# The state read of an attention-and-experts kernel in 64x32 tiles over two banks, beside the small S.W group, with one ring of eight PSUM banks

## The chip, the cores and the metric

The kernel runs on one core of a Trainium2 chip. The metric is device time in microseconds (us) of one execution; the numbers are medians over several executions. A core has TensorE (PE in the profile; its weight loads are listed as PEld), VectorE (DVE), ScalarE (ACT), GpSimd (POOL) and SyncE (SP, which issues most DMAs). Matmul results land in PSUM, eight banks of 128 partitions with 512 float32 columns each, and VectorE or ScalarE copies ("evicts") them to SBUF.

## The reference

For each of 8 batches and 8 heads, `x` has 512 tokens of 64 features and `state` has 32 rows of 64. Both read each other with softmax attention; the two reads are laid one after the other as 544 rows per batch, heads side by side in 512 columns, and go through a two-expert layer with a maximum:

```python
scores = scale * np.matmul(x, state.transpose(0, 1, 3, 2))
a = softmax(scores)                        # over the 32 state rows
xread = np.matmul(a, state)
scores2 = scale * np.matmul(state, x.transpose(0, 1, 3, 2))
a2 = softmax(scores2)                      # over the 512 tokens
sread = np.matmul(a2, x)
attn = np.concatenate([xread, sread], axis=2)
...
h1 = attn_rows @ w1
h2 = attn_rows @ w2
out = np.maximum(h1, h2) @ w_out
```

(`softmax` stands for the lines that subtract the maximum, take the exponential and divide by the sum.) Inputs and output are float32; `w1` and `w2` are 512x1024, `w_out` is 1024x512.

## The kernel before

max(h1, h2) is computed as h2 + relu(h1 - h2): `wd` holds w1 - w2, `wo` holds w_out, and `wwo` holds w2 @ w_out. Since the rows of xread are a @ state, the kernel multiplies each batch's state by the weights first. In its names, for a batch `b`:

- `sc_mm`, `sc_ev`: the scores and their exponentials `e` (ScalarE, L233). `norm` (L237 to L241) divides by the sums; the result `a` is transposed by a DMA into `aT`.
- `sw_mm` (L309), the small S.W group: state times `wd` and `wwo`, in three blocks of 512 columns. Each block is 8 matmuls of 64 rows by 32 columns of weights, into two banks; 24 matmuls in all. `sw_ev` copies the six banks into `sw`, three by VectorE and three by ScalarE (L97, L95).
- `l1` (L339): 8 tiles of two matmuls, `sw` against `aT`, with the relu on ScalarE (L328) and VectorE (L330) in turn.
- `l2(b, c)` (L349 and L354): for each of 4 blocks of 128 tokens, two matmuls against the `wwo` part of `sw` and eight against `wo`; `l2_out` copies the bank to `h` (c even on VectorE, odd on ScalarE), and `store` writes four blocks out.
- `sr_mm` (L275), the state read: 32 matmuls per batch, weights `e` (128 rows, 32 columns, one of four column groups of the array), moving `xe` (65 columns: 64 features and a one, which gives the sum of the exponentials). All accumulate in one bank: 4 heads on the partitions, two head groups of 65 columns, or 130 columns per batch. `sr_ev` (L283 to L289) takes the reciprocal of the sums and scales; `sr_tr` (L293) transposes `sr`, and `sr_cp` puts it into `sread_t`, which is multiplied by the weights at the end (`m1`, `m2`).

The first stage, batch 0 and the weights, follows a written order (`ORDER`). After it comes a loop over b = 1 to 6, the passes, which issues in program order on each engine. Pass b does l1 of batch b, scores of batch n = b + 1, l2(0) and l2(1) of b, S.W of n, the state read, the evictions of both, l2(2), l2(3) and the transposes of sr. In pass 1 l1, the scores, l2(0) and l2(1) lie in the written order already. Passes 1 and 2 read two states each: `rd` is (n, b - 1). In the loop, banks come from two rings: "r" with banks 0 to 5 for l1, scores, S.W and the transposes, and "a" with banks 6 and 7 for l2 and the state read. A matmul that opens a bank waits until the bank's last contents have been read. After the loop batch 7 runs l1, `m1` and three blocks of l2 into held banks; a branch on a flag (sums out of range) guards a slower path, which these inputs do not take.

The order in the loop around the change:

```python
        pg = [sw_mm(n, 512 * z, 512 * z + 512) for z in range(3)]
        rd = (n, b - 1) if b < 3 else (n,)
        p = bank("a")
        for j, v in enumerate(rd):
            sr_mm(v, p, j)
        for z in range(3):
            sw_ev(pg[z], n, 512 * z, 512 * z + 512, "VA" if z % 2 == 0 else "AV")
        for j, v in enumerate(rd):
            sr_ev(p[:, 130 * j:130 * j + 130], v, "VA"[j])
```

Of the kernel before, what the change touches and what calls it, by code (L numbers as in the profile page):

```python
# [8 lines left out]
F32 = mybir.dt.float32  # L9
# [3 lines left out]
ALU = mybir.AluOpType  # L13
# [31 lines left out]
def kernel(  # L45
# [9 lines left out]
    nc = tc.nc  # L55
# [3 lines left out]
    DM = H * D  # L59
    FF = moe_w1.shape[1]  # L60
    NC = S // 128
# [22 lines left out]
    def bank(ring="r", dtype=F32):  # L84
        if isinstance(ring, int):
            i = ring
        else:
            r = rings[ring]
            i = r[turn[ring] % len(r)]
            turn[ring] += 1  # L90
        return banks[i] if dtype == F32 else banks[i].bitcast(BF16)
# [175 lines left out]
        copy(eng, at_tile(b)[:, g].rearrange("p c t -> p (c t)"), p[:, 0:512])  # L267


    def sr_mm(b, p, j=0):  # L270
        d = d_(b)
        for c in range(NC):
            for g in range(2):
                for k in range(4):
                    nc.tensor.matmul(p[32 * k:32 * k + 32, 130 * j + 65 * g:130 * j + 65 * g + 65], d["e"][:, g, c, k],  # L275
                                     d["xe"][:, c, k, 7 + 65 * g:72 + 65 * g],
                                     start=(j == 0 and c == 0 and g == 0), stop=(c == NC - 1 and g == 1),
                                     skip_group_check=True)

    def sr_ev(p, b, eng="V"):  # L280
        sr = at.tile([128, 2, D], BF16, tag="sr", bufs=3, name="sr")
        d_(b)["sr"] = sr
        nc.vector.reciprocal(rr_all[:, b], p[:, 0:130:129])  # L283
        for g in range(2):
            o, i, r = sr[:, g, :], p[:, 1 + 64 * g:65 + 64 * g], rr_all[:, b, g:g + 1]
            if eng == "A":
                nc.scalar.activation(out=o, in_=i, func=ACTF.Copy, scale=r)  # L287
            else:
                nc.vector.tensor_scalar(o, i, scalar1=r, scalar2=None, op0=ALU.mult)  # L289
# [67 lines left out]
    def l2_out(b, c, p, eng, lo=0, hi=DM):  # L357
        if b not in OB:
            OB[b] = h8(NC, DM)
        copy(eng, OB[b][:, c, lo:hi], p[:, lo:hi])  # L360

    def l2(b, c, eng=None, ring="a"):
        p = bank(ring)
        l2_open(b, c, p, True, False)
        l2_f(b, c, p, range(NF), False, True)
        l2_out(b, c, p, eng or ("A" if c % 2 else "V"))

    def store(b, c0=0, c1=NC, lo=0, hi=DM, eng=None):
        dst = out[b * L:b * L + S].rearrange("(p c) n -> p c n", c=NC)
# [76 lines left out]
    ps = {}  # L446
# [74 lines left out]
        step(tok)  # L521


    rings["r"], rings["a"] = [0, 1, 2, 3, 4, 5], [6, 7]
    turn["r"] = turn["a"] = 0
    for b in range(1, B - 1):
        n = b + 1
        if b > 1:
            if b + 2 < B:
                for g in range(2):  # L530
                    cast_b(b + 2, g, "P")
                xt_dma(b + 2)
            for f in range(NF):
                l1(b, f)
            pp = [sc_mm(n, hh) for hh in range(2)]
            for hh in range(2):
                sc_ev(pp[hh], n, hh)
            for hh in range(2):
                norm(n, hh, "P")
            at_dma(n)  # L540
        else:
            for g in range(2):
                cast_b(3, g, "P")
            xt_dma(3)
        if b > 2 and b + 2 < B:
            for k in range(4):
                cast_e(b + 2, k, "P")
        if b + 3 < B:
            for g in range(2):
                load_x(b + 3, g)  # L550
        if b > 1:
            l2(b, 0)
            l2(b, 1)
        pg = [sw_mm(n, 512 * z, 512 * z + 512) for z in range(3)]
        rd = (n, b - 1) if b < 3 else (n,)
        p = bank("a")
        for j, v in enumerate(rd):
            sr_mm(v, p, j)
        for z in range(3):
            sw_ev(pg[z], n, 512 * z, 512 * z + 512, "VA" if z % 2 == 0 else "AV")  # L560
        for j, v in enumerate(rd):
            sr_ev(p[:, 130 * j:130 * j + 130], v, "VA"[j])
        if b < 3:
            for k in range(4):
                cast_e(b + 2, k, "P")
        l2(b, 2)
        if n == B - 1:

            cl = at.tile([128, B * 34], F32, tag="cl", bufs=1, name="cl")
            ne = at.tile([128, B * 34], F32, tag="ne", bufs=1, name="ne")  # L570
            bad = at.tile([128, 1], BF16, tag="bad", bufs=1, name="bad")
            flag = at.tile([128, 1], I32, tag="flag", bufs=1, name="flag")
            sv = sums[:, 0:B * 34]
            nc.vector.tensor_scalar(cl, sv, scalar1=1e-20, scalar2=1e20, op0=ALU.max, op1=ALU.min)
            nc.vector.tensor_tensor(ne, cl, sv, op=ALU.not_equal)
            nc.vector.tensor_reduce(bad, ne, axis=AXX, op=ALU.max)
        l2(b, 3)
        for v in rd:
            sr_cp(sr_tr(v, "r"), v, "A")
        if n == B - 1:  # L580
            p = bank("r")
            nc.tensor.matmul(p[0:2, 0:1], ones, bad, start=True, stop=True)
            nc.vector.tensor_copy(flag[0:1, :], p[0:1, 0:1])
        store(b)
# [16 lines left out]
    with tc.If(nc.values_load(flag[0:1, 0:1], skip_runtime_bounds_check_because="compared with zero alone") >= 1):  # L601
        mx = at.tile([128, 2 * NC, 2], F32, tag="mx", bufs=1, name="mx")
        cm = at.tile([64, 2], F32, tag="cm", bufs=1, name="cm")
        e2 = at.tile([64, 512], BF16, tag="e2", bufs=1, name="e2")
        gx, gob, gd = h8(H, NC * D), h8(NC, DM), h8(NC, DM)
        dl = gd[:, 0, :]
        for v in range(B):
            st[v], AT[v], SW[v], R[v], xf_t[v] = st[b], AT[b], SW[b], R[b], gx
            if v < b:
                OB[v] = gob  # L610
            d = d_(v)
            for g in range(2):
                fetch_x(v, 4 * g, 4 * g + 4)
            for k in range(4):
                cast_e(v, k, "AV"[k % 2])
            for k in range(4):
                xt_ev(xt_mm(v, k), v, k, "AV"[k % 2])
            for hh in range(2):
                pv = sc_mm(v, hh).rearrange("p (c g i n) -> p g c i n", c=NC, g=2, i=2)
                for g in range(2):  # L620
                    m = mx[:, 4 * g:4 * g + 4]
                    dv = dl[:, 256 * g:256 * g + 256].rearrange("p (c i n) -> p c i n", c=NC, i=2)
                    nc.vector.tensor_reduce(m, pv[:, g], axis=AXX, op=ALU.max)
                    nc.vector.tensor_tensor(dv, pv[:, g], m.unsqueeze(3).to_broadcast([128, NC, 2, Ns]),
                                            op=ALU.subtract)
                nc.scalar.activation(out=e_view(v, hh), in_=dl.rearrange("p (m i n) -> p m i n", i=2, n=Ns),
                                     func=ACTF.Exp, scale=scale)
                norm(v, hh, "V")
            for g in range(2):
                at_ev(at_mm(v, g, "r"), v, g, "AV"[g])  # L630
            for k in range(4):
                p = bank("r")
                for c in range(NC):
                    nc.tensor.matmul(p[0:64, c * 128:(c + 1) * 128], sbd[:, v, k, :], d["xt"][:, c, k, :],
                                     start=(c == 0), stop=(c == NC - 1))
                nc.vector.tensor_reduce(cm[:, 0:1], p[0:64], axis=AXX, op=ALU.max)
                nc.vector.tensor_scalar(cm[:, 1:2], cm[:, 0:1], scalar1=-scale, scalar2=None, op0=ALU.mult)
                nc.scalar.activation(out=e2, in_=p[0:64], func=ACTF.Exp, bias=cm[:, 1:2], scale=scale)
                pt = bank("r", BF16)
                for c in range(NC):  # L640
                    nc.tensor.transpose(pt[:, c * 64:(c + 1) * 64], e2[:, c * 128:(c + 1) * 128], ident[0:64, 0:64])
                copy("V", d["e"][:, :, :, k, :], pt[:, 0:256].rearrange("p (c g n) -> p g c n", c=NC, g=2))
            p = bank("r")
            sr_mm(v, p)
            sr_ev(p, v)
            sr_cp(sr_tr(v, "r"), v, "A")
            for z in range(3):
                sw_ev(sw_mm(v, 512 * z, 512 * z + 512), v, 512 * z, 512 * z + 512)
            for f in range(NF):
                l1(v, f)  # L650
            if v < b:
                for c in range(NC):
                    l2(v, c, ring="r")
                store(v)
        for f in range(NF):
            m1(f)
        l2_held()
# [42 lines left out]
```

## Time and profile before

| | |
|---|---|
| Time, median of 3 runs | 151.7 us (150.84 to 152.78) |
| Time of the profiled execution | 152.39 us |
| Its span, first to last instruction | 150.6 us |
| Granted TensorE clock, mean | 0.993 |
| Busy: TensorE, its weight loads | 139.7 us, 70.4 us |
| Busy: VectorE, ScalarE, GpSimd | 84.8 us, 65.9 us, 50.8 us |

The profile is of one execution. Its timeline has a line for each run of like instructions: start in us from the span's start, length in us, engine, line of the kernel, operation, what it writes and reads, shape, count, and in brackets how long the engine had been idle and what ended that. The length reaches from the first start to the last end, and since matmuls are pipelined the next line's start can lie before it. Lines of groups have busy time in us and mean ns of one instruction, then the idle time before them. Below, S marks the start of the last matmul of l2(1) in a pass.

### The profile page before, as it was taken

To read this page: it belongs to the slowest core of one execution; us is meant where nothing else is said; L and a number is where in the kernel's file an instruction comes from. 1 tells how busy PE (TensorE), PEld (TensorE's weight loads), DVE (VectorE), ACT (ScalarE), POOL (GpSimd) and SP (SyncE) were. 2 spreads that over 40 slices of the span, in tenths; PEclk is the share of its full clock that TensorE was granted. 3 is DMA by queue.
4 is the path that set the end of the run, shared out by engine and by line. 5 is a ranking of instruction groups with operands and counts; after the bars stand their busy time and mean duration, and the time that the engine had idled before them with its cause. 6 is when DMAs were issued, how large, how long until landed. Compare 5 with 4: busy or idle time off the path is not lost. (4 is left out here: it accounts for less than half of the span.)

```text
span 150.6 us, 3166 instructions
## 1 busy us (share of the span) xinstructions
PE 139.7 (93%) x1262; PEld 70.4 (47%) x1281; DVE 84.8 (56%) x167; ACT 65.9 (44%) x129; POOL 50.8 (34%) x71
## 2 busy tenths in 40 slices
PE   6769899999999999999999999999999999998970
PEld 2446445544444445444544544454445444843450
DVE  3579787964717828563854676284838575502120
ACT  5233663664682546246540825371455417401100
POOL 3123223499002932862490556228201300000000
PEclk9999999999999999999999999999999999999997
DMA  4999999946916399899979977995823305000541
GB/s 106 297 371 362 362 351 360 340 105 109 264 52 279 72 140 354 275 138 362 281 133 212 343 144 71 282 318 100 74 120 159 60 16 246 35 11 7 209 172 41
DMA packets 36741, 29.11 MB, mean 193 GB/s; under 512 B 21616, under 2 KB 34160, under 8 KB 35824
## 3 DMA queue, kind: packets, MB, share of 16 engines
q1 hardware_dynamic: 36304, 28.64, 68.7%
q8 instruction: 12, 0.20, 0.5%
q10 hardware_dynamic: 416, 0.20, 0.5%
q14 instruction: 9, 0.07, 0.2%
HBM read 15.20 MB, written 8.91 MB: 160 GB/s over the span
## 5 line engine op out<-in xcount | busy, mean ns | idle before, releaser
L354 PE MATMUL bank<-wo,r 128*128 128x512 bf16 (+1 forms) x261 | 61.3, 373 | 0.6 <-issue 0.2
L354 PEld LDWEIGHTS <-r 128*128 128x128 bf16 x264 | 25.5, 98 | 28.9 <-issue 0.7
L95 ACT COPY h<-bank 128x512 f32<-128x512 f32 (+1 forms) x17 | 9.5, 574 | 48.3 <-PE bank L354 37.8
L339 PE MATMUL bank<-aT,sw 128*128 128x512 bf16 x128 | 30.1, 379 | 0.1
L330 DVE TENSOR_SCALAR r<-bank 128x512 bf16<-128x512 f32 x28 | 19.4, 692 | 17.5 <-PE bank L339 16.9
L328 ACT ACTIVATE r<-bank 128x512 bf16<-128x512 f32 x36 | 21.3, 612 | 7.3 <-PE bank L339 7.0
L241 POOL TENSOR_TENSOR a<-e,er 128x512 bf16<-128x512 bf16 x13 | 13.4, 1048 | 27.4 <-ACT e L233 15.6
L97 DVE CAST sw<-bank 128x512 bf16<-128x512 f32 (+1 forms) x25 | 15.1, 653 | 11.5 <-PE bank L309 11.5
L99 POOL CAST xb<-h 128x1024 bf16<-128x1024 f32 x12 | 12.4, 1039 | 18.5 <-issue 12.0
L339 PEld LDWEIGHTS <-sw 128*128 128x128 bf16 x128 | 12.0, 98 | 12.9
L99 POOL CAST xe<-h 128x512 bf16<-128x512 f32 x27 | 15.8, 622 | 6.5 <-DMA h<-in_x_dram 5.7
L97 DVE COPY h<-bank 128x512 f32<-128x512 f32 (+1 forms) x16 | 10.5, 659 | 12.4 <-PEq L601 6.5
L349 PE MATMUL bank<-sw,aT 128*128 128x512 bf16 (+1 forms) x53 | 16.1, 372 | 0.5 <-ACT sr L287 0.2
L95 ACT CAST sw<-bank 128x512 bf16<-128x512 f32 (+1 forms) x27 | 13.2, 559 | 6.2 <-PE bank L309 6.2
L233 ACT ACTIVATE e<-bank 128x512 bf16<-128x512 f32 x16 | 8.9, 595 | 5.5 <-PE bank L225 4.9
L237 DVE TENSOR_REDUCE sums<-e 128x16 f32<-128x512 bf16 x16 | 10.6, 663 | 1.1 <-ACT e L233 1.0
L426 PE MATMUL bank<-wo,w2t 128*128 128x512 bf16 x30 | 7.8, 380 | 0.8 <-DVE w2t L97 0.6
L433 PE MATMUL bank<-wz 128*128 128x256 bf16 (+1 forms) x38 | 7.4, 337 | 1.2 <-DVE ones L438 1.2
L349 PEld LDWEIGHTS <-aT 128*128 128x128 bf16 x66 | 5.5, 98 | 4.8 <-issue 0.7
L225 PEld LDWEIGHTS <-xt 128*128 128x128 bf16 x128 | 5.0, 98 | 2.1 <-ACT xt L95 0.3
L309 PE MATMUL bank<-wd,sbd 64*32 64x512 bf16 (+1 forms) x144 | 5.6, 358 | 0.0
L99 POOL CAST wo<-h 128x1024 bf16<-128x1024 f32 x3 | 3.1, 1039 | 7.1 <-DMA h<-in_moe_w_out_dram 7.1
(71 smaller groups left out, 110.3 us busy)
## 6 DMA issues: line engine op xcount, KB each, us to landing
h<-in_x_dram SPq DMA_DIRECT2D x14, 512.0 KB, 5.5
out_dram<-h SPq DMA_DIRECT2D x7, 1024.0 KB, 4.2
h<-in_moe_w_dram SPq DMA_DIRECT2D x8, 512.0 KB, 9.3
h<-in_moe_w_out_dram SPq DMA_DIRECT2D x4, 512.0 KB, 9.3
h<-in_x_dram SPq DMA_DIRECT2D x4, 256.0 KB, 4.1
out_dram<-h SPq DMA_DIRECT2D x3, 256.0 KB, 2.4
out_dram<-rs SPq DMA_DIRECT2D x2, 256.0 KB, 2.4
sf<-in_state_dram SPq DMA_DIRECT2D x1, 384.0 KB, 9.0
```

Source lines behind the costliest of these rows:

```text
L95: nc.scalar.copy(o, i)
L97: nc.vector.tensor_copy(o, i)
L99: nc.gpsimd.tensor_copy(o, i)
L233: nc.scalar.activation(out=e_view(b, hh).rearrange("p (g c) i n -> p g c (i n)", g=2), in_=p.rearrange("p (c g m) -> p g c m", c=NC, g=2), ...
L237: nc.vector.tensor_reduce(es_all[:, b, hh], e_view(b, hh), axis=AXX, op=ALU.add)
L241: (nc.gpsimd if eng == "P" else nc.vector).tensor_mul(e_view(b, hh, "a"), e_view(b, hh), d_(b)["er"][:, hh].unsqueeze(3).to_broadcast([128 ...
L328: nc.scalar.activation(out=o, in_=p, func=ACTF.Relu)
L330: nc.vector.tensor_scalar(o, p, scalar1=0.0, scalar2=None, op0=ALU.max)
L339: nc.tensor.matmul(p, SW[b][:, g, f * 128:(f + 1) * 128], AT[b][:, g].rearrange("p c t -> p (c t)"), start=(g == 0), stop=(g == 1))
L349: nc.tensor.matmul(p[:, lo:hi], AT[b][:, g, c, :], SW[b][:, g, FF + lo:FF + hi], start=(start and g == 0), stop=(stop and g == 1))
L354: nc.tensor.matmul(p[:, lo:hi], R[b][:, f, c * 128:(c + 1) * 128], wo[:, f, lo:hi], start=(start and j == 0), stop=(stop and j == len(fs) ...
L426: nc.tensor.matmul(p, w2t[:, f, i, :], wo[:, f, :], start=(f == 0), stop=(f == NF - 1))
```

## The change

The state read is split by rows: each of its 32 matmuls becomes two of 64 rows, one into each of two banks (`pr`), so that its tiles have the shape of the S.W group. It is issued before S.W, right behind l2(1). A new `sr_add` copies the second bank to SBUF with ScalarE and adds the first to it with VectorE; `sr_ev` then reads the sum from SBUF. It stands before the S.W evictions in the queues of both engines. In the loop and after it all banks come from one ring of eight, in the order in which they are asked for. The eviction of l2(1) is split: VectorE copies columns 0 to 255 and ScalarE the rest. Lines of the new kernel are shifted: the state read is L279, S.W L319, l2 L359 and L364, the copy and the add L286 and L287.

```diff
--- before.py
+++ after.py
@@ -86,6 +86,8 @@
             i = ring
         else:
             r = rings[ring]
+            if len(r) == 8:
+                ring = "r"
             i = r[turn[ring] % len(r)]
             turn[ring] += 1
         return banks[i] if dtype == F32 else banks[i].bitcast(BF16)
@@ -267,15 +269,23 @@
         copy(eng, at_tile(b)[:, g].rearrange("p c t -> p (c t)"), p[:, 0:512])
 
 
-    def sr_mm(b, p, j=0):
+    def sr_mm(b, ps, j=0):
         d = d_(b)
         for c in range(NC):
             for g in range(2):
                 for k in range(4):
-                    nc.tensor.matmul(p[32 * k:32 * k + 32, 130 * j + 65 * g:130 * j + 65 * g + 65], d["e"][:, g, c, k],
-                                     d["xe"][:, c, k, 7 + 65 * g:72 + 65 * g],
-                                     start=(j == 0 and c == 0 and g == 0), stop=(c == NC - 1 and g == 1),
-                                     skip_group_check=True)
+                    for r in range(2):
+                        h = slice(64 * r, 64 * r + 64)
+                        nc.tensor.matmul(ps[r][32 * k:32 * k + 32, 130 * j + 65 * g:130 * j + 65 * g + 65],
+                                         d["e"][h, g, c, k], d["xe"][h, c, k, 7 + 65 * g:72 + 65 * g],
+                                         start=(j == 0 and c == 0 and g == 0), stop=(c == NC - 1 and g == 1),
+                                         skip_group_check=True)
+
+    def sr_add(ps, n):
+        half = at.tile([128, 260], F32, tag="srh", bufs=1, name="srh")
+        nc.scalar.copy(half[:, 0:130 * n], ps[1][:, 0:130 * n])
+        nc.vector.tensor_tensor(half[:, 0:130 * n], ps[0][:, 0:130 * n], half[:, 0:130 * n], op=ALU.add)
+        return half
 
     def sr_ev(p, b, eng="V"):
         sr = at.tile([128, 2, D], BF16, tag="sr", bufs=3, name="sr")
@@ -363,7 +373,10 @@
         p = bank(ring)
         l2_open(b, c, p, True, False)
         l2_f(b, c, p, range(NF), False, True)
-        l2_out(b, c, p, eng or ("A" if c % 2 else "V"))
+        eng = eng or "VA"[c % 2]
+        w = DM // len(eng)
+        for z, e in enumerate(eng):
+            l2_out(b, c, p, e, w * z, w * z + w)
 
     def store(b, c0=0, c1=NC, lo=0, hi=DM, eng=None):
         dst = out[b * L:b * L + S].rearrange("(p c) n -> p c n", c=NC)
@@ -521,7 +534,7 @@
         step(tok)
 
 
-    rings["r"], rings["a"] = [0, 1, 2, 3, 4, 5], [6, 7]
+    rings["r"] = rings["a"] = list(range(8))
     turn["r"] = turn["a"] = 0
     for b in range(1, B - 1):
         n = b + 1
@@ -550,12 +563,13 @@
                 load_x(b + 3, g)
         if b > 1:
             l2(b, 0)
-            l2(b, 1)
+            l2(b, 1, "VA")
+        rd = (n, b - 1) if b < 3 else (n,)
+        pr = [bank() for r in range(2)]
+        for j, v in enumerate(rd):
+            sr_mm(v, pr, j)
+        p = sr_add(pr, len(rd))
         pg = [sw_mm(n, 512 * z, 512 * z + 512) for z in range(3)]
-        rd = (n, b - 1) if b < 3 else (n,)
-        p = bank("a")
-        for j, v in enumerate(rd):
-            sr_mm(v, p, j)
         for z in range(3):
             sw_ev(pg[z], n, 512 * z, 512 * z + 512, "VA" if z % 2 == 0 else "AV")
         for j, v in enumerate(rd):
@@ -640,9 +654,9 @@
                 for c in range(NC):
                     nc.tensor.transpose(pt[:, c * 64:(c + 1) * 64], e2[:, c * 128:(c + 1) * 128], ident[0:64, 0:64])
                 copy("V", d["e"][:, :, :, k, :], pt[:, 0:256].rearrange("p (c g n) -> p g c n", c=NC, g=2))
-            p = bank("r")
-            sr_mm(v, p)
-            sr_ev(p, v)
+            pr = [bank() for r in range(2)]
+            sr_mm(v, pr)
+            sr_ev(sr_add(pr, 1), v)
             sr_cp(sr_tr(v, "r"), v, "A")
             for z in range(3):
                 sw_ev(sw_mm(v, 512 * z, 512 * z + 512), v, 512 * z, 512 * z + 512)
```

## The prediction

> **What bounds the kernel now.** I read the page's busy table and slices first, then the timeline of one loop pass (b = 3), then the instruction groups with shapes kept apart, for prices.
>
> ```profile
> span 150.6 us, 3166 instructions
> ...
> PE 139.7 (93%) x1262; PEld 70.4 (47%) x1281; DVE 84.8 (56%) x167; ACT 65.9 (44%) x129; POOL 50.8 (34%) x71
> ...
> PE   6769899999999999999999999999999999998970
> ...
> PEclk9999999999999999999999999999999999999997
> ```
>
> From the fourth slice to the last few the TensorE row is at nine tenths and the granted clock does not fall, so time can only come out of, or go into, the spacing of matmuls. The other engines are half idle; they matter where a matmul waits for them. One pass around the place of the change:
>
> ```profile
> 75.33 1.89 PE L354 MATMUL bank<-wo,r 128*128 128x512 bf16 x8
> ...
> 77.16 0.62 PE L309 MATMUL bank<-wd,sbd 64*32 64x512 bf16 x16
> 77.26 0.58 ACT L95 COPY h<-bank 128x512 f32<-128x512 f32 x1 [3.46 <-PE bank L354]
> 77.60 0.40 PE L309 MATMUL bank<-wwo,sbd 64*32 64x512 bf16 x8
> 77.63 1.89 DVE L97 CAST sw<-bank 128x512 bf16<-128x512 f32 x3 [1.83 <-PE bank L309]
> ...
> 77.92 0.43 PE L275 MATMUL bank<-xe,e 128*32 128x65 bf16 x32
> 78.29 0.39 PE L349 MATMUL bank<-sw,aT 128*128 128x512 bf16 x1
> ```
>
> Full 128x512 matmuls follow each other every 0.216 us. The last of l2(1) starts at 76.84 (75.33 + 1.89 less its own 0.38); call that S. The S.W group (L309) starts at S + 0.31, so 0.09 over the 0.216 pitch. Its 24 matmuls of 64x32 tiles run eight at a time in three rounds of 0.216 (+0.01). The state read (L275) starts 0.765 after it instead of 0.66: 0.11 lost where the tile shape goes from 64x32 to 128x32. Its 32 matmuls run four at a time in eight rounds of 0.032 us; after them another 0.10 is lost before l2(2) opens at 78.29 = S + 1.445. (One record of the pair that opens l2(2) is missing; the next line starts two pitches later.) So each pass pays about 0.1 us at each of three changes of tile shape, and TensorE waits for nobody.
>
> Passes 1 and 2 read two states each, and there another engine does hold TensorE:
>
> ```profile
> 49.12 0.69 PE L275 MATMUL bank<-xe,e 128*32 128x65 bf16 x64
> ...
> 50.19 1.89 PE L354 MATMUL bank<-wo,r 128*128 128x512 bf16 x8
> ...
> 51.70 0.52 ACT L287 ACTIVATE sr<-bank,sums 128x64 bf16<-128x64 f32 x2 [0.92 <-DVE sums L283]
> ...
> 52.27 0.59 PE L349 MATMUL bank<-sw,aT 128*128 128x512 bf16 x2 [0.19 <-ACT sr L287]
> ```
>
> l2(3) takes the bank of the state read, which is freed by sr_ev, queued behind the sw evictions: the step from the last L354 start to L349 is 0.57 in pass 1 and 0.34 in pass 2 instead of 0.216, so 0.35 and 0.13 lost.
>
> ```profile
> L95 ACT COPY h<-bank 128x512 f32<-128x512 f32 x16 | 9.2, 587 | 44.1 <-PE bank L354 33.6 <-PEq L601 7.0 <-POOL xe L99 2.5
> L95 ACT COPY h<-bank 128x256 f32<-128x256 f32 x1 | 0.4, 372 | 4.2 <-PE bank L354 4.2
> L289 DVE TENSOR_SCALAR sr<-bank,sums 128x64 bf16<-128x64 f32 x12 | 2.9, 280 | 0.2
> L97 DVE COPY h<-bank 128x256 f32<-128x256 f32 x1 | 0.4, 425 | 0.5 <-PE bank L354 0.5
> L575 DVE TENSOR_TENSOR ne<-cl,sums 128x272 f32<-128x272 f32 x1 | 0.4, 443 | 0.0
> ```
>
> These are the prices of the new evictions, below.
>
> **The change, part by part.**
>
> *Removed: one change of tile shape per pass.* State read and S.W share 64x32, so TensorE goes 128x128, 64x32, 128x128: entry 0.09 as now, nothing between, exit 0.115 (the S.W groups of the first stage, straight into 128x128 tiles, show it: at 37.74 the step to the next matmul is 0.308). Gain 0.10 per pass, 0.6 us over six, if nothing waits.
>
> *Added: 64 matmuls per state where there were 32.* Eight tiles instead of four, each with the same 65 columns. The trace has no 64x32 matmul this short. From below: in S.W, same tile, two banks, starts are 3.4 ns apart, so a round of eight needs 0.027 us. From the nearest row that is slow, today's state read: one pair of load and matmul per 7.9 ns (64 pairs in 0.50 us in pass 1), so 0.063 a round if pairs cannot go faster than that. From far above: the score matmuls (L225, full tiles, 64 columns) start every 29 ns, so 0.23 a round. I take 0.032 a round, 4 ns a pair: S.W is the nearest row (same tile, same two banks in parallel), and the 65 columns set 0.032 in today's rounds, since within each the four start within 10 ns and then 20 ns pass. Then eight rounds cost 0.256, the same as now.
>
> *Moved: the state read goes ahead of S.W.* Its inputs are early: e is written at 72.7 to 73.8, xe a pass before (the casts for state 2 ended at 37.8, its read is at 49.1). No DMA is moved past another. POOL's xe casts of passes 1 and 2, which follow the read, are released some 0.7 earlier, which nothing on TensorE asks for.
>
> *Added: a copy, an add, and with them a wait.* With the ring of eight, l2(2) takes the bank of the first half of the sum, so its first matmul waits for the VectorE add, which waits for the ScalarE copy, which waits for the state read. For passes 3 to 6, from S: last state matmul starts 0.31 + 7 x 0.032 + 0.025 = 0.56, ends 0.19 later at 0.75; ScalarE starts 0.04 later (l2(1) ends at 77.22, its copy starts at 77.26) at 0.79, and is free, as its half of l2(1) runs from 0.42 to 0.79; copying 130 columns 0.27 (372 ns at 256, 0.83 ns a column between 256 and 512) to 1.06; 0.03 to VectorE (e to its reduction: 73.31 to 73.34); add of 130 columns 0.30 (between 280 ns at 64 and 443 at 272) to 1.39; 0.05 back to TensorE (sr to L349: 52.22 to 52.27) gives **S + 1.44**. TensorE alone would be there at 0.31 + 0.256 + 0.66 + 0.115 = S + 1.34. So the gain of 0.10 turns into a wait of 0.10: 1.44 against 1.445 now.
> The Trainium skill, TensorEngine Tiling, section Performance Considerations (PSUM Bottleneck), says that tiling speeds TensorE but not the emptying of PSUM, which can become the bound: by it the end is S + 1.44, without it S + 1.34; no run here shows which yet.
>
> *Passes 1 and 2*, sixteen rounds and 260 columns: last start 0.31 + 15 x 0.032 + 0.025 = 0.815, end 1.01, copy 1.05 to 1.42, add (0.43) 1.45 to 1.88, l2(2) at S + 1.93; TensorE alone 1.60. Now l2(2) opens at S + 1.705 and l2(3) loses 0.35 or 0.13, together 2.06 and 1.83; the new l2(3) takes the other half's bank, free at 1.42, and no longer waits. So -0.13 and +0.10.
>
> *The rest of the ring and the split of l2(1).* The third S.W round takes the bank of l2(1), hence the split: both halves are out at S + 0.84, the round starts at about S + 1.0. VectorE has 0.425 more from the half and 0.30 from the add, and sw evictions start at S + 1.39 instead of 0.79 (77.63): the last of three (0.60 apart) and sr_ev end near 80.8 instead of 80.1. Behind them stand the transpose of sr at 82.6 and the next l1 at 82.7; the two l2 tiles hide this with 1.8 us to spare, and without them it would cost 0.7. Other banks come round after eight allocations, longer than before. In the tail each accumulator's bank is copied out over 2 us before it comes round. I cost these at nothing.
>
> **Sum.** Passes 3 to 6: 4 x (1.44 - 1.445) = -0.02; passes 1 and 2: -0.03. Together -0.05 us on a profiled execution of 152.39 (span 150.6 and 1.8 around it). That one lies 0.7 above the median of the runs, 151.7, and I take the difference over: **151.6 us**, no change.
>
> **The rivals.**
>
> *A: the wait is not there*, because copy and add are shorter or hand over faster. For: the handovers are read to 0.01 us only. Against: copy and add would have to shrink by 0.10 of 0.57 in four passes and 0.33 of 0.80 in two. Gain 4 x 0.10 + (1.83 - 1.60) + (2.06 - 1.60) = 1.1 us: 150.6.
>
> *B: the doubled pairs are fed no faster than now*, 7.9 ns each, at L279 of the new kernel, and the wait behind moves with them. For: no row shows 128 loads and matmuls in 0.25 us; S.W's burst is of 16. Against: the 20 ns pauses inside today's rounds. Then the last start is S + 0.81, its end 1.00, l2(2) at 1.69: +0.245 in four passes; in two, last start 1.31, l2(2) at 2.43: +0.37 and +0.60. Together +1.95: 153.6. It decides from 4.1 ns a pair on, and passes 2% (3.0 us) from about 10 ns.
>
> *C: row halves do not overlap at all* and each pair costs L225's 29 ns: a state takes 1.86 us instead of 0.25, +1.6 in each of four passes and +3.2 in each of two, 12.6 in all: 164. For: only a different tile shows it. Against: S.W's eight tiles side by side.
> The Trainium skill, TensorEngine Tiling, section Instruction Overhead, gives about 60 cycles to each matmul however few its columns, and warns against tiling a dimension that is already small; by it, if singly paid at 2.4 GHz, 256 more matmuls would cost an estimated 6.4 us, or 158. This trace's 7.9 ns a pair shows that column tiles share it; no run shows whether row halves do.
>
> **How the numbers follow.** Forecast 0.58, A 0.14, B 0.18, C 0.04, and 0.06 for a wait that the ring makes where I see none. The likeliest alone spans 151.0 to 152.3 (0.1 us of handover in six passes either way). The range reaches to A and B, with 0.3 us for the scatter of a median whose runs lie from 150.84 to 152.78: 150.3 to 153.9. Faster by over 2% would need 3 us where only 1.1 is idle: 0.02. Slower by over 2% is C, half of the unseen wait and the far end of B: 0.13. Within 2%, about what a measurement of this kernel can tell from no change: 0.85.
>
> **What would show it.** In the profile after: no step above 0.03 between state read and S.W; eight rounds of 0.032 (B: 0.063); ScalarE's copy near S + 0.79, the add ending near S + 1.39, and l2(2) some 0.05 after the add with VectorE named as its releaser (A: l2(2) at S + 1.34, no wait); in passes 1 and 2 no wait at l2(3). I am wrong if l2(2) opens outside S + 1.35 to S + 1.55 in passes 3 to 6, or if l1, the transposes of sr or the tail show a wait.

## The result, and the profile after

The changed kernel takes 153.82 us (median of 6 runs, 153.25 to 154.77) against 151.5 us before (6 runs). The ratio is 1.0138, with a 95% interval of 1.0097 to 1.0179: slower by 2.1 to 2.3 us, within the 2% that the prediction called no change, but clear of 1. Ratios here and below leave out executions in a slower state of the chip, so they can differ a little from the quotient of two medians. The profiled execution took 153.6 us, with this page:

```profile
span 151.7 us, 3710 instructions
...
PE 142.9 (94%) x1537; PEld 73.8 (49%) x1537; DVE 87.7 (58%) x178; ACT 66.5 (44%) x135; POOL 51.2 (34%) x71
...
PEclk9999999999999999999999999999999999999999
```

TensorE is as full as before and its clock is whole. What changed is the spacing of the matmuls around the state read. The timeline of pass 3 after (start in us, length in us, then as before):

```profile
78.11 0.57 PEld L279 LDWEIGHTS <-e 64*32 64x32 bf16 x64 [0.42 <-issue]
78.11 0.69 PE L279 MATMUL bank<-xe,e 64*32 64x65 bf16 x64
78.22 0.42 DVE L99 COPY h<-bank 128x256 f32<-128x256 f32 x1 [1.47 <-PE bank L364]
...
78.61 0.66 PE L319 MATMUL bank<-wd,sbd 64*32 64x512 bf16 x16
78.68 0.37 ACT L97 COPY h<-bank 128x256 f32<-128x256 f32 x1 [3.92 <-DVE h L99]
...
79.01 0.27 ACT L286 COPY srh<-bank 128x130 f32<-128x130 f32 x1
79.05 0.46 PE L319 MATMUL bank<-wwo,sbd 64*32 64x512 bf16 x8
...
79.31 0.29 DVE L287 TENSOR_TENSOR srh<-bank,srh 128x130 f32<-128x130 f32 x1 [0.66 <-ACT srh L286]
...
79.66 0.59 PE L359 MATMUL bank<-sw,aT 128*128 128x512 bf16 x2
```

S, the start of l2(1)'s last matmul, is 77.80 here. Three things are to be seen. The starts of the read's matmuls span 0.49 (78.11 to 78.60) where 0.26 was expected. ScalarE's half of l2(1) does not run beside VectorE's but after it: the bracket names VectorE's write of `h` as what it waited for. And l2(2) opens at 79.66, S + 1.85, right behind the add. In all six passes it opens 0.05 after the add's end, and in passes 1 and 2 its idle time is long enough to stand in the list of TensorE's waits (us in total, times, longest):

```profile
PE bank L359 <- DVE srh L287: 0.8, 2, 0.4
```

The single starts of the read show where its 0.49 goes. A pair is a weight load and its matmul; the times are those of the matmuls, in us after the first:

| | pair 32 | pair 33 | pair 64 |
|---|---|---|---|
| after, pass 3 | 0.129 | 0.228 | 0.487 |
| after, pass 1 (128 pairs) | 0.129 | 0.228 | 0.486 |
| before, pass 1 (64 pairs) | 0.239 | 0.259 | 0.497 |

After the change 32 pairs go at 4.2 ns each, then comes a hole of 0.099 without a start, and then 8.3 ns a pair.

The next table gives l2(2)'s start after S, read from the single starts; for before, passes 1 and 2 include what l2(3) then lost.

| pass | before | predicted | after |
|---|---|---|---|
| 1 | 2.06 | 1.93 | 2.57 |
| 2 | 1.83 | 1.93 | 2.68 |
| 3 | 1.445 | 1.44 | 1.85 |
| 4, 5, 6 | 1.44 to 1.45 | 1.44 | 1.80 |

The six differences make 2.82 us. TensorE's last matmul starts 2.26 later than before (147.97 against 145.71): the first stage happened to be 0.38 shorter in this execution, the wait at the branch 0.11, and the step behind l2(2)'s first matmul 0.01 in each pass. The spans differ by 1.1 only, since in the profiled execution of before the last store landed in 3.0 us and in this one in 1.9. So the whole loss lies in these stretches; nowhere else in the loop is a step longer than before.

### The profile page after: what moved, and what is told of

The parts are those of the page before. It is cut to its first block, busy times and chain, and to the rows that moved or that the text cites. A ratio compares the mean times of both kernels' runs of the same rounds, so it can differ in the third digit from the quotient of the medians.

```text
span 151.7 us, 3710 instructions
## 1 busy us (share of the span) xinstructions
PE 142.9 (94%) x1537; PEld 73.8 (49%) x1537; DVE 87.7 (58%) x178; ACT 66.5 (44%) x135; POOL 51.2 (34%) x71
## 5 line engine op out<-in xcount | busy, mean ns | idle before, releaser
L364 PE MATMUL bank<-wo,r 128*128 128x512 bf16 (+1 forms) x264 | 61.8, 373 | 0.0
L364 PEld LDWEIGHTS <-r 128*128 128x128 bf16 x264 | 25.4, 98 | 28.9 <-issue 0.7
L97 ACT COPY h<-bank 128x512 f32<-128x512 f32 (+1 forms) x17 | 8.5, 511 | 47.5 <-DVE h L99 19.4
L99 DVE COPY h<-bank 128x512 f32<-128x512 f32 (+1 forms) x21 | 12.6, 602 | 16.3 <-PE bank L364 7.7
L359 PE MATMUL bank<-sw,aT 128*128 128x512 bf16 (+1 forms) x66 | 18.9, 372 | 1.2 <-DVE srh L287 0.8
L359 PEld LDWEIGHTS <-aT 128*128 128x128 bf16 x66 | 5.9, 98 | 6.9 <-issue 2.5
L319 PE MATMUL bank<-wd,sbd 64*32 64x512 bf16 (+1 forms) x144 | 5.8, 357 | 0.0
L279 PEld LDWEIGHTS <-e 64*32 64x32 bf16 x512 | 4.5, 89 | 2.6 <-issue 2.5
```

Of the source, the lines that this page charges most:

```text
L97: nc.scalar.copy(o, i)
L99: nc.vector.tensor_copy(o, i)
L359: nc.tensor.matmul(p[:, lo:hi], AT[b][:, g, c, :], SW[b][:, g, FF + lo:FF + hi], start=(start and g == 0), stop=(stop and g == 1))
L364: nc.tensor.matmul(p[:, lo:hi], R[b][:, f, c * 128:(c + 1) * 128], wo[:, f, lo:hi], start=(start and j == 0), stop=(stop and j == len(fs) ...
```

## The experiments

Two theories came out of the two profiles. F: instructions come to TensorE too slowly for the state read, which has twice as many now ("the feeding"); its rival R says that the array sets the pace, by columns or by row halves. H: the two halves of l2(1)'s eviction run one after the other, and ScalarE's copy of the state read stands behind them; its rivals are that the split costs nothing, or that copy and add are the whole loss. The ring of eight was to be told apart from both. The times below are beside runs of the kernel before on the same chip; l2(2) is given after S.

**One engine for l2(1).**

```diff
-            l2(b, 1, "VA")
+            l2(b, 1, "V")
```

> The changed kernel with l2(1) evicted whole by VectorE instead of in two halves. Theory H (one bank is read by one engine at a time, so ScalarE's half of l2(1) starts only when VectorE's has ended, and its copy of the state read stands behind it): without the split ScalarE is idle when the state read ends, the copy starts 0.04 to 0.16 us after that, at S + 1.03 to 1.15 instead of 1.2, and l2(2) opens at S + 1.68 to 1.80 instead of 1.80 to 1.85 in passes 2 to 6: 0.2 to 0.7 us less than the changed kernel, ratio to before about 1.010. Rival F alone (the state read is fed too slowly, and the split costs nothing): l2(2) stays at S + 1.80, ratio 1.014.

Measured: ratio 1.0118 (1.0074 to 1.0162). l2(2) at 1.72 in passes 4 to 6, 1.84 in pass 3, 2.57 and 2.62 in passes 1 and 2. Pass 4 in the timeline (S = 92.77):

```profile
93.08 0.69 PE L279 MATMUL bank<-xe,e 64*32 64x65 bf16 x64
93.18 0.69 DVE L99 COPY h<-bank 128x512 f32<-128x512 f32 x1 [1.44 <-PE bank L364]
...
93.84 0.27 ACT L286 COPY srh<-bank 128x130 f32<-128x130 f32 x1 [4.06 <-PE bank L279]
```

ScalarE is idle for 4 us and now waits for the state read itself. The split cost 0.08 a pass in passes 4 to 6, 0.30 in all by the trace; the time's interval is too wide to tell that from nothing. Most of the loss is still there.

**The halves in the other order.**

```diff
-        for z, e in enumerate(eng):
+        for z, e in reversed(list(enumerate(eng))):
```

> The changed kernel with the halves of l2(1) issued in the other order: ScalarE's before VectorE's. Theory H (one bank is read by one engine at a time): now VectorE's half waits for ScalarE's and starts near S + 0.83, ScalarE's starts at S + 0.42, the copy of the state read follows its end, and l2(2) opens at S + 1.68 to 1.80. Without H both halves start near S + 0.42.

Measured: 153.92 us, one run. The timeline of pass 4 (S = 92.58):

```profile
92.99 0.37 ACT L97 COPY h<-bank 128x256 f32<-128x256 f32 x1 [3.40 <-PE bank L364]
...
93.40 0.43 DVE L99 COPY h<-bank 128x256 f32<-128x256 f32 x1 [1.84 <-ACT h L97]
93.65 0.27 ACT L286 COPY srh<-bank 128x130 f32<-128x130 f32 x1 [0.28 <-PE bank L279]
```

Now VectorE waits for ScalarE, 0.03 after its end, and l2(2) opens at 1.72. So whichever comes second waits. In both orders the second half's instruction waits for the other engine's semaphore, so it is the program that orders them. That it does so for the shared bank and not for the shared tile in SBUF is an argument, not a test: the S.W evictions of both engines write one tile `sw` at the same time, out of different banks.

**Fewer columns.**

```diff
-                        nc.tensor.matmul(ps[r][..., 130 * j + 65 * g:130 * j + 65 * g + 65], d["e"][h, g, c, k],
-                                         d["xe"][h, c, k, 7 + 65 * g:72 + 65 * g],
+                        lo, hi = (0, 65) if c == 0 else (32 * g, 32 * g + 33)
+                        nc.tensor.matmul(ps[r][..., 130 * j + 65 * g + lo:130 * j + 65 * g + hi], d["e"][h, g, c, k],
+                                         d["xe"][h, c, k, 7 + 65 * g + lo:7 + 65 * g + hi],
```

> The changed kernel with 33 instead of 65 columns in three quarters of the state read's matmuls (half of the features of the later token blocks are left out); as many instructions as before. Theory F (the feeding of instructions sets the pace: 64 go ahead, then a hole of 0.1 us, then one per 4.2 ns): the set still takes 0.49 us, with 8.3 ns a pair in its second half. Rival R (the array sets it, by its columns): the second half runs at about 4.2 ns a pair and the set takes 0.36 us.

Measured: 153.58 us, one run. The set takes 0.487 in passes 3 to 6, as with 65 columns, with 0.126 at pair 32 and 0.229 at pair 33, and after that each pair takes 8.3 ns in both. The columns of these later matmuls were halved and nothing moved: columns do not set the pace there.

**Half of the pairs.**

```diff
-        for c in range(NC):
+        for c in range(NC // 2):
```

> The changed kernel with half of the state read left out (two of four token blocks): 32 pairs per state. Theory F: in passes 3 to 6 all 64 instructions are at hand, so the set takes 0.135 us, 4.2 ns a pair, with no hole in it; the hole moves into S.W. In passes 1 and 2, with 64 pairs, the hole is after pair 32. Rival R (row halves can't keep 4 ns a pair): 0.25 us, 7.7 ns a pair.

Measured: 152.56 us, one run. Pass 3 (S = 76.82):

```profile
77.12 0.20 PEld L279 LDWEIGHTS <-e 64*32 64x32 bf16 x32 [0.42 <-issue]
77.12 0.32 PE L279 MATMUL bank<-xe,e 64*32 64x65 bf16 x32
77.23 0.42 DVE L99 COPY h<-bank 128x256 f32<-128x256 f32 x1 [1.47 <-PE bank L364]
...
77.35 0.66 PE L319 MATMUL bank<-wd,sbd 64*32 64x512 bf16 x16
77.69 0.37 ACT L97 COPY h<-bank 128x256 f32<-128x256 f32 x1 [3.92 <-DVE h L99]
```

32 pairs start within 0.13 us, 4.2 ns a pair, and the 0.10 hole now stands between them and S.W (77.25 to 77.35). In pass 1, with 64 pairs, it comes after pair 32 again. So 64 instructions are at hand when the read starts (65 with the load of pair 33, which still goes ahead of the hole), whatever comes behind them, and then one comes every 4.17 ns. The next matmul starts 0.23 after the first, be it that of the read's pair 33 or S.W's first. In pass 1 of before the end of the burst lies at the same place: the load of pair 34 starts 0.236 after the first matmul (0.232 after the change), and from there the loads stand 8.3 ns apart. The first 32 pairs took 0.24 there, so no hole was to be seen. But l2(2) stays at 1.80 in passes 3 to 6, which no theory had said: the chain VectorE's half, ScalarE's half, copy, add (0.42 to 1.75) does not ask when the read ends. With copy and add in place, the split and the slow read each suffice to keep l2(2) late in passes 4 to 6, at 1.80 and 1.72, and lie side by side. In passes 1 to 3 the read decides: with one engine for l2(1), l2(2) came only 0.00, 0.06 and 0.01 earlier there.

**The state read behind S.W.**

```diff
-            l2(b, 1, "VA")
+            l2(b, 1)
...
-        for j, v in enumerate(rd):
-            sr_mm(v, pr, j)
-        p = sr_add(pr, len(rd))
         pg = [sw_mm(n, 512 * z, 512 * z + 512) for z in range(3)]
+        pr = [bank() for r in range(2)]
+        for j, v in enumerate(rd):
+            sr_mm(v, pr, j)
         for z in range(3):
             sw_ev(...)
+        p = sr_add(pr, len(rd))
```

> The changed kernel with the state read behind S.W again (64x32 tiles, two banks, copy and add kept; l2(1) whole on ScalarE). l2(2) now takes the bank of the first S.W block, so it doesn't wait for the add. Theory F (the read costs 0.49 instead of 0.26 us a state): l2(2) at S + 1.60 to 1.66 in passes 3 to 6, about S + 2.1 in passes 1 and 2, no wait at l2(3): about 1.2 us more than before, ratio 1.008. If the copy and add were the whole loss: S + 1.37, ratio 0.995.

Measured: ratio 1.0051 (1.0022 to 1.0081), l2(2) at 1.66 in passes 3 to 6, 2.30 and 2.19 in passes 1 and 2, l2(3) without a wait. Here l2(2) does not depend on the add, and 0.22 a pass is lost all the same. It comes from the read, whose second pair also waits 0.09 for l2(1)'s bank, until ScalarE's whole copy of it has ended. With the copy and the add off the path and l2(1) undivided, about half of the change's loss is left by the trace (1.5 of 2.8 us), and somewhat less by the times.

**Without the add.**

```diff
-            l2(b, 1, "VA")
+            l2(b, 1)
...
-        nc.scalar.copy(half[:, 0:130 * n], ps[1][:, 0:130 * n])
-        nc.vector.tensor_tensor(half[:, 0:130 * n], ps[0][:, 0:130 * n], half[:, 0:130 * n], op=ALU.add)
+        nc.vector.tensor_copy(half[:, 0:130 * n], ps[0][:, 0:130 * n])
```

> The changed kernel with l2(1) whole on ScalarE and the second half of the sum left out: the add is a single VectorE copy of the first bank, and nobody reads the second. The wait for two engines in a row is gone. Theory F: TensorE alone sets l2(2), S + 1.58 in passes 3 to 6 (0.31 + 0.495 + 0.66 + 0.115), 0.13 more than before. If the chain of copy and add were all: S + 1.34.

Measured: ratio 1.0056 (1.0025 to 1.0087), l2(2) at 1.61 in passes 3 to 6, where 1.58 was expected for TensorE alone. Against the kernel with one engine for l2(1), 1.72, copy and add cost 0.11 a pass in passes 4 to 6; the other 0.17 over before is what the longer read costs, less the gain of one change of tile shape.

**The read in two pieces around the first S.W round** (second half of the sum left out, as above).

```diff
+        pieces = [(v, j, cs) for j, v in enumerate(rd) for cs in (range(2), range(2, NC))]
+        for z in range(3):
+            for v, j, cs in pieces[z:z + 1]:
+                sr_mm(v, pr, j, cs)
+            ...
+            pg.append(sw_mm(n, 512 * z, 512 * z + 512))
```

> As the kernel without the add (second half of the sum left out, l2(1) whole on ScalarE), with the state read in two pieces of 32 pairs, the first before the first S.W round and the second behind it. Theory F: while a round of S.W streams for 0.22 us the queue fills again, both pieces run at about 4 ns a pair and l2(2) opens at S + 1.35 to 1.47, less than the S + 1.58 of the undivided read. Rival R: dividing changes nothing, S + 1.58.

Measured: ratio 1.0159 (1.0108 to 1.0211), l2(2) at 1.65 to 1.76 in passes 3 to 6, and at 2.87 in passes 1 and 2. The expectation failed. The first piece runs at 4.2 ns a pair, S.W's first round comes after the hole, and the second piece, from S + 0.75, has 24 quick pairs, then four at 8.3 ns, a hole of 0.06 and again 8.3 ns a pair; its last matmul starts at 1.035 instead of 0.80. The time while the round streams was not enough for 64 instructions to be at hand again, and VectorE's copy of the later read then holds l2(2). How instructions arrive while TensorE waits is left open.

**Both costs out.** Half of the pairs, l2(1) on ScalarE, one copy instead of copy and add.

> The changed kernel with both costs taken out: half of the state read left out (32 pairs a state), l2(1) whole on ScalarE, and one VectorE copy in place of copy and add (second half of the sum left out). If the feeding of instructions and the wait behind the add are the whole loss: the set takes 0.13 us, a hole of 0.1 us before S.W, and l2(2) opens at S + 1.35 to 1.45 in passes 3 to 6, no later than before. If something else in the new order costs: S + 1.5 or later.

Measured: 151.01 us, one run, the lowest of the kernels that read in 64x32 tiles. l2(2) at 1.39 in passes 3 to 6, as expected:

```profile
90.57 0.32 PE L279 MATMUL bank<-xe,e 64*32 64x65 bf16 x32
...
90.80 0.66 PE L318 MATMUL bank<-wd,sbd 64*32 64x512 bf16 x16
91.06 0.29 DVE L286 COPY srh<-bank 128x130 f32<-128x130 f32 x1 [1.82 <-PE bank L279]
...
91.65 0.39 PE L358 MATMUL bank<-sw,aT 128*128 128x512 bf16 x1
```

S is 90.26. Besides the 0.10 in the hole, one more cost shows: the second matmul of the third S.W round starts 0.09 after the first, since it waits until ScalarE has copied the undivided l2(1) out of the bank that it takes (the trace names that copy as the releaser). This is the wait that the split was meant to spare. Even with both, l2(2) opens 0.05 earlier than before, so slow read, split and late add together are enough to explain the loss in these passes.

**The ring of eight alone**, on the kernel before, twice.

```diff
-    rings["r"], rings["a"] = [0, 1, 2, 3, 4, 5], [6, 7]
+    rings["r"] = rings["a"] = list(range(8))
```

> The kernel before with one change only: one ring of eight banks. State read, order and evictions as before. If the ring is harmless and lifts the wait of l2(3) in passes 1 and 2: 0.48 us less than before (0.35 + 0.13), ratio 0.997, l2(2) at S + 1.445 in passes 3 to 6 as before. If the ring itself costs the changed kernel its time: ratio 1.005 to 1.014, with new waits at l1 or S.W.

> The kernel before with the ring of eight alone, timed again beside the one above. The wait of l2(3) in passes 1 and 2 (0.48 us in the profile of before) gone, and a wait at l1 of pass 3 that differs from execution to execution in its place: ratio 0.994 to 1.000.

Measured: ratios 0.9977 (0.9948 to 1.0006) and 0.9984 (0.9941 to 1.0026). The waits of l2(3) are gone (steps of 0.216 in all passes), and no wait at a bank is new. But in both profiles l1 of pass 3 waits for the transposed `a`, as in the second one's waits of TensorE (us in total, times, longest):

```profile
PE bank L341 <- DMA aT<-a: 0.4, 1, 0.4
```

The steps from the last transpose of sr to l1 are 1.00 and 0.64 instead of 0.06. The transposes were issued at 64.17 and 63.65 and landed 4.9 later, at 69.04 and 68.56, and l1 started 0.04 after that. In before, the transpose issued at 63.60 landed at 68.45, 0.4 ahead of its l1 at 68.83. So it had 0.4 to spare, and TensorE came to l1 0.7 and 0.8 earlier: 0.48 of that is what l2(3) no longer loses, the rest a first stage that was 0.21 and 0.35 shorter in these executions. In the first profile the transpose was also issued 0.57 later. So the gain met a new wait. Neither interval excludes no change.

**The ring, and `a` first in pass 2.**

```diff
-            if b + 2 < B:
+            if 2 < b < B - 2:
                 for g in range(2):
                     cast_b(b + 2, g, "P")
                 xt_dma(b + 2)
...
             at_dma(n)
+            if b == 2:
+                for g in range(2):
+                    cast_b(b + 2, g, "P")
+                xt_dma(b + 2)
```

> The kernel before with the ring of eight, and in pass 2 GpSimd normalises a and its transpose is issued before the casts and the transpose of the batch after next. In the profile of the ring alone l1 of pass 3 waited 0.9 us for that transpose of a (issued at 64.2, needed at 68.1). If that wait is what is left of the ring's gain: issued about 1 us or more earlier, no wait at l1 in pass 3, 0.5 to 1.4 us less than before, ratio 0.991 to 0.997. If the late issue is not the cause: as the ring alone, 0.998.

Measured: ratio 0.9962 (0.9929 to 0.9995): 0.4% faster than before, small but clear of 1. SyncE's queue in that pass:

```profile
61.82 1.24 SPq L259 DMA_TRANSPOSE aT<-a  x1
63.78 3.11 SPq L204 DMA_TRANSPOSE xt<-xb  x1
```

The transpose of `a` goes out 2.4 earlier than in the first profile of the ring (64.2), lands at 64.86, and l1 of pass 3 follows the last transpose of sr at 0.06: the wait is gone. This version is faster than both kernels. Its interval overlaps that of the ring alone, so the times do not show apart what moving `a` is worth.

## Why the prediction was wrong

- **The step that failed first is the price of the added pairs.** The prediction took 0.032 a round, 4 ns a pair, so that 64 pairs would cost what 32 cost now. That holds for the first 32: eight pairs per 35 ns or so. Then comes a hole of 0.099 and after it 8.33 ns a pair. The last state matmul starts at S + 0.80 instead of 0.56 in passes 3 to 6, and at 1.33 and 1.38 instead of 0.815 in passes 1 and 2. In passes 1 to 3, with 1.8 of the 2.8 us, this read is what the copy waited for. The two halves of a round overlap, so the price from S.W's burst of 16 instructions was right for the array and wrong for what feeds it.
- **Rival B had the right pace and nearly the right sum**: 7.9 ns a pair, l2(2) at 1.69 and 2.43, 153.6 us in all; measured 7.7 to 8.5, 1.80 and 2.6, and 153.8. It got 0.18. That the sum came out so near is in part luck: its 7.9 ns is close to the mean of quick pairs, hole and slow pairs, and it left the split of l2(1) out; with one engine for l2(1), the passes 4 to 6 did open at 1.72. The argument against it, the 20 ns pauses in the rounds of before, was read from the wrong part. In pass 1 of before, 64 pairs at a stretch, the weight loads of the last 30 pairs stand 8.3 ns apart, after a denser start; four of them make 33 ns, just what a round of four took, so the end of the burst was hidden. It could have been read before the run.
- The Trainium skill, TensorE: Matmul & The Clock Gate, gives TensorE a queue of 64 instructions (in its table of specifications). The trace agrees to within one instruction: the hole stands after 32 pairs and one more load, with 65 or 33 columns. By the 60 cycles a matmul of the Trainium skill, TensorEngine Tiling (section Instruction Overhead), singly paid as in the prediction's estimate, a pair would have taken an estimated 25 ns; measured are 4.2 and then 8.3.
- **The second step that failed is the split of l2(1).** "Both halves are out at S + 0.84" was 1.25: the program lets one engine empty the bank after the other. In passes 4 to 6 ScalarE's copy of the state read stood right behind its late half, and the run with half of the pairs shows that this suffices there: with a read of 0.13, l2(2) still opened at 1.80.
- The Trainium skill, PSUM — Partial Sum Buffer, section on PSUM bank collisions, says that two engines must not touch one bank and the same partitions at a time, and that the compiler's scheduler therefore makes one wait for the other, reads too. Both orders of the halves agree, with 0.03 from the end of the one to the start of the other.
- **Handover to ScalarE.** Expected 0.23 from the last state matmul's start to the copy. With ScalarE free (one engine for l2(1)) it was 0.28 in passes 4 to 6 and 0.35 to 0.40 in passes 1 to 3. Why more there stays open. The copy (0.27 and 0.38), the add (0.30 and 0.43) and the steps behind them were as priced.
- **The mechanism of the wait was right**: l2(2) opens 0.05 after the add, with the add named as its releaser, and the gain of the tile shape becomes a wait. Counted along the read, the 0.36 above the predicted 1.44 in passes 4 to 6 is 0.24 from the read, 0.05 from the handover and 0.07 from the split. This is one way to share it out: taking the long read away alone gains nothing there, and taking the split away alone gains 0.08.
- **Right as well**: no step between state read and S.W beyond the feeding (0.008), l2(3) without a wait, and no wait at l1, the transposes of sr or the tail. Rival A did not occur; C is excluded by the first 32 pairs.

## What to carry to other kernels

Before splitting small matmuls, count instructions and not only columns: the dense burst here ran at the array's pace for 64 instructions, and at the pace at which instructions came after that, and a longer burst of the same engine elsewhere in the trace shows where that begins. A result spread over two banks has to be put together, here by two engines in a row, and where all banks are in one ring the next tile waits for it. Splitting an eviction between two engines gains nothing if both halves lie in one bank and the program lets one wait for the other: here 0.83 us for both halves against 0.59 for the whole by ScalarE. When a wait is taken off a full engine, look for what arrives next: here a DMA that had about 0.4 us to spare.

## What the runs showed of the hardware that was not expected

- TensorE started 64 instructions (32 loads with their matmuls) within 0.13 us, then nothing for 0.097 to 0.104, then one per 4.17 ns. The place of the hole went by the number of instructions: after pair 32 of 64 or 128, and between read and S.W where the read had 32 pairs. The first matmul behind the hole started 0.227 to 0.229 after the first of the burst in all these cases.
- After a round of S.W of 0.216 us, not 32 but 24 pairs of the read's second piece went fast.
- Where S.W follows the read in the same tile shape, its first matmul starts 0.008 after the last of the read; with a change of shape, 0.31 after the last start in place of 0.216.
